# Batch 0's last couple in a fused attention and maxout kernel: two gate operations move ahead of four form operations, and one staged load moves behind two block turns

## The chip, the cores and the metric

The kernel runs on one core of a Trainium2 chip. The metric is device microseconds of that core, from the first to the last moment of one execution; several runs are taken and their median counts. A profile is one further execution, recorded instruction by instruction.

## The reference

For each of 8 batches, with S = 3072 tokens, D = 256 and 64 columns in z, a gated attention unit without softmax is computed, and its output goes through a maxout layer:

```python
scores = (1.0 / S) * np.matmul(z, z.transpose(0, 2, 1))
attn = np.maximum(scores, 0.0) ** 2
x = (u * np.matmul(attn, v)).reshape(B * S, D)          # 24576 x 256
out = np.maximum(x @ w1, x @ w2) @ w_out                # d_ff = 1024
```

All inputs and the output are float32 in HBM; the matmuls run in bf16.

## The kernel before

**Tiles.** The 3072 queries of a batch form six groups of 512, and a couple is two neighbouring groups, so a batch has three couples. The squared scores of one query group against four key tiles (512 keys) are a *block*, 128 partitions by 4 x 512 in bf16. Scores are symmetric, so only blocks with key index at or above the query index are computed; the others are *turned* copies, made by a DMA transpose (`mirror`, L279). There are 27 block buffers for everything. They stand in a list, `free`: `Block()` takes the first (L81), and `release()` puts a buffer at the end (L97). Both happen while the program is written out, not while it runs: `mirror` releases its source as soon as the turn has been put on the queue's list, and a later owner of that buffer gets a semaphore wait for the turn that still has to read it.

**Scores.** `score_pair` (L223) makes half a block: two matmuls into two of four PSUM banks (L237), ReLU by ScalarE into one of three `r_sb` buffers (L250; in every third pair of group 3 one half is done by VectorE, L248), and a square by VectorE into the block (L260). In group 3 of batch 0 one such pair is emitted at every fourth step of the attention matmuls (L297), and the pairs are those that later groups need.

**Batch 0.** Groups 0 to 3 are computed plainly (L297). Groups 4 and 5, batch 0's last couple, go by seven products of block sums (L1149), whose operands are *forms*: VectorE adds and subtracts whole blocks (L335, made by `prepare`, L337). For this couple `prepared(2)` gives 14 operations as `early`: eight on v (L193 to L196) and then, for the two forms, s3, s3, s1, s1, s2, s2. Each s1 reads a turned block. The *gate* of a group (L465, two operations for 512 queries) multiplies the attention output by the turned u and gives the feed-forward's input. Between group 3 and the couple, TensorE runs the feed-forward of couple 0 (L632 inner, L654 outer products).

**Order around the change.** Every engine runs its own list in order. SyncE's queue (SP) issues all turns, the staged loads and the stores. A staged load (`u_staged`, L207, and `z_staged`, L144, through `staged`, L129) takes a block buffer as float32 landing place, issues the load on SP, and has GpSimd cast it to bf16 (L142, L148). In group 3 (`i == 3`) the steps run over key tiles n; `u_staged(0, 5)` stands at n = 1, `z_staged` at n = 4, and a held-back turn (`later`) at n = 0, 4, 8, 12 and so on. After group 3, `sums` and the first `first` operations of `early` go to VectorE, then the gate of group 3, then the rest of `early`:

```python
        first = 4 * NC + len(forms)
        second(PLAIN // 2 - 2, sums + early[:first])
        xTs[b, g], gates = gate(b, g, {dc: h[0] for dc, h in halves.items()})
        for do in gates + early[first:]:
            do()
```

Here NC is 3 and there are two forms, so `first` is 14 and all of `early` stands ahead of the gate.

Of the kernel before, what the change touches and what calls it, by code (L numbers as in the profile page):

```python
# [11 lines left out]
def kernel(  # L12
# [26 lines left out]
    NC = NG // 2  # L39
# [79 lines left out]
    def zT_pe(lo, n, copies):  # L119
        tp = mm_tile([P, n, P], bf16, "tpz")[0]  # L120
        for j in range(n):
            nc.tensor.transpose(tp[:, j, :], z_bf16(lo + j - 1, 2), ident)  # L122
        at = 0
        for copy, k in copies:
            copy(zT[:, lo + at : lo + at + k, :], tp[:, at : at + k, :])
            at += k
        assert at == n
# [13 lines left out]
    def load_staged(dst, src):  # L141
        nc.gpsimd.tensor_copy(dst, staged(dst, src))  # L142
# [68 lines left out]
    def turn_u(b, g):  # L211
        t = upool.tile([P, G, KD, P], bf16, name="uT")
        nc.sync.dma_start_transpose(
            t.rearrange("p a c r -> p (a c) r"), un[b, g].rearrange("p a d -> p (a d)")
        )
        uT[b, g] = t
# [75 lines left out]
    def attn_unit(b, g, t, acc, dc, first, last):  # L292
        blk, j = divmod(t, G)
        a = A[b, g, blk]
        for half in range(2):
            rows = ds(half * R, R)
            nc.tensor.matmul(  # L297
                a.out(acc[half, dc]),
                v_at(b, t, dc)[rows],
                a.moving(rows, j),  # L300
                start=first,
                stop=last,
            )
        if dc == KD - 1 and j == G - 1:
            a.release()
# [4 lines left out]
    def drain(acc, dcs):  # L310
        hs = {}
        for dc in dcs:
            hs[dc] = new_h()
            nc.scalar.copy(hs[dc], acc[1, dc])
        for dc in dcs:
            nc.vector.tensor_add(hs[dc], hs[dc], acc[0, dc])
        return hs

    def drain_fast(acc, dc):
        hs = [new_h() for half in range(2)]  # L320
        nc.scalar.copy(hs[1], acc[1, dc])
        nc.vector.tensor_copy(hs[0], acc[0, dc])
        return hs
# [138 lines left out]
    def gate(b, g, hs):  # L462
        x = xpool.tile([P, KD, GW], bf16, name="xT")
        return x, [
            lambda dc=dc: nc.vector.scalar_tensor_tensor(  # L465
                out=x[:, dc, :].rearrange("p (t r) -> p t r", r=P),
                in0=hs[dc].rearrange("p (t r) -> p t r", r=P),
                scalar=c2,
                in1=uT[b, g][:, :, dc, :],
                op0=ALU.mult,  # L470
                op1=ALU.mult,
            )
            for dc in range(KD)
        ]
# [289 lines left out]
    def emit_pair(wait=0, shared=False, act=False):  # L764
        nonlocal done
        shared = shared or done < 12 and done % 3 == 0
        finish = score_pair(
            *pairs[done], dve_half=1 if shared else None, halves=done == 0, act=act
        )
        done += 1  # L770
        if wait:
            due.append((tick + wait, finish))
        else:
            finish()

    def flush(now=None):
        while due and (now is None or due[0][0] <= now):
            due.pop(0)[1]()
# [6 lines left out]
    def steps_of(i):  # L785
        tiles, both = range(NT), range(KD)
        head = edge(i - 1) if i else 0
        tail = NT - edge(i)
        steps = [(n, dc) for dc in both for n in tiles[:head]]
        steps += [(n, dc) for n in tiles[head:tail] for dc in both]  # L790
        return steps + [(n, dc) for dc in both for n in tiles[tail:]]
# [9 lines left out]
    def need(b, g, n):  # L801
        most = pair_at[b, g, 2 * g]
        for t in range(n + 1):
            if t // G >= g:
                most = max(most, pair_at[b, g, t // 2] + 1)
        return most

    with tc.manual_schedule():
# [21 lines left out]
        def by_chunk(w):  # L830
            return w.rearrange("(c p) f -> p c f", p=P)
# [32 lines left out]
        for i in range(PLAIN):  # L864
# [6 lines left out]
            for slot, (n, dc) in enumerate(steps_of(i)):  # L871
                k = need(b, g, n)
                upto = max(k, min(done + 1, k + AHEAD)) if slot in slots else k
                while done < min(upto, len(pairs)):
                    emit_pair(
                        wait=int(i < 2 and slot == slots[-1]), shared=i == 3 and done % 3 == 1
                    )
                if i == 0 and slot in (8, 22):
                    if slot == 8:
                        zT_pe(12, 8, [(nc.scalar.copy, 4)] * 2)  # L880
                    else:
                        zT_pe(20, 5, [(nc.scalar.copy, 5)])
                    if slot == 22:
                        for x in z_first:
                            x.release()
                attn_unit(b, g, n, acc, dc, n == 0, n == NT - 1)
                if n == NT - 1 and i < PLAIN - 1:
                    if i < 2:
                        new[dc] = drain_fast(acc, dc)
                        flush()  # L890
                    else:
                        new.update(drain(acc, [dc]))
                if dc:
                    continue
                if i in (1, 2) and n in (6, 9):
                    h = sums[n // 9]
                    nc.vector.tensor_add(h[0], h[0], h[1])
                    sums[n // 9] = h[0]
                if i and n == 12:
                    xTs[groups[i - 1]], tasks = gate(*groups[i - 1], sums)  # L900
                if i and n in (12, 15):
                    tasks[n // 15]()
                if i == 0 and n == 14:
                    turn_u(0, 0)
                if (i, n) == (0, 16):
                    turn_u(0, 1)
                if (i, n) == (0, 20):
                    nc.vector.memset(w2_sb[:, 0, 0:1], 0.0)
                    nc.gpsimd.dma_start(out=w2_sb, in_=by_chunk(moe_w2))
                if (i, n) == (1, 9):  # L910
                    w1_32 = [staged(w2_sb[:, c : c + 1], by_chunk(moe_w1)[:, c : c + 1]) for c in range(KD)]
                if (i, n) == (1, 11):
                    u_staged(0, 2)
                if (i, n) == (1, 13):
                    for h in range(2):
                        part = slice(h * KF // 2, (h + 1) * KF // 2)
                        load_staged(w_out_sb[:, part], by_chunk(moe_w_out)[:, part])
                if (i, n) in ((1, 15), (2, 14), (3, 4)):
                    z_staged(1, i - 1)
                if (i, n) == (2, 2):  # L920
                    turn_u(0, 2)
                if (i, n) == (2, 5):
                    u_staged(0, 3)
                if (i, n) == (2, 17):
                    turn_u(0, 3)
                if (i, n) in ((2, 18), (3, 1)):
                    u_staged(0, 4 + (i > 2))
                if (i, n) in ((2, 10), (3, 10)):
                    turn_z(1, i - 2)
                if (i, n) == (3, 16):  # L930
                    turn_z(1, 2)
                if later and n % 4 == 0 and (i == 3 or i and n > 12):
                    later.sort(key=lambda block: (block[2] > 3, block[1], block[2]))
                    mirror(*later.pop(0))
                if i == 2 and n == 16:
                    for c in range(KD):
                        nc.vector.tensor_sub(w15_sb[:, c : c + 1], w1_32[c], w2_sb[:, c : c + 1])
                if i == 2 and n in (15, 18):
                    half = n // 18
                    tp = mm_tile([P, KF, P], bf16, "tpw")[0]  # L940
                    for j in range(KF):
                        nc.tensor.transpose(tp[:, j, :], w2_sb[:, half, ts(j, P)], ident)
                    nc.scalar.copy(w2T_sb[:, half, :, :], tp)
                if i == 2 and n == 18:
                    w2.release()
# [66 lines left out]
        sums = [lambda h=h: nc.vector.tensor_add(h[0], h[0], h[1]) for h in halves.values()]  # L1012
        loads_behind(PLAIN // 2 - 1)
        forms, early, last_v, late = prepared(PLAIN // 2)
        first = 4 * NC + len(forms)
        second(PLAIN // 2 - 2, sums + early[:first])
        xTs[b, g], gates = gate(b, g, {dc: h[0] for dc, h in halves.items()})
        for do in gates + early[first:]:
# [3 lines left out]
        for i in range(PLAIN // 2, len(couples)):  # L1022
# [4 lines left out]
                b, c, forms, blocks=() if b else (q2, q1)  # L1027
# [102 lines left out]
            for s, pair in enumerate(steps):  # L1130
# [9 lines left out]
                for half, (name, w, blk, j) in enumerate(pair):  # L1140
                    rows = ds(half * R, R)
                    bank = BANK[name]
                    first = bank not in opened
# [28 lines left out]
            if i + 1 < len(couples):  # L1172
                forms, early, last_v, late = prepared(i + 1)
# [43 lines left out]
```

## Time and profile before

| | us |
|---|---|
| median of three runs | 902.83 (902.02 to 903.13) |
| the profiled execution itself | 904.61 |
| its span, first to last instruction | 902.6 |
| TensorE busy | 892.0 (99%) |
| VectorE busy | 741.7 (82%) |
| ScalarE busy | 722.6 (80%) |
| GpSimd busy | 95.4 (11%) |

Times inside the trace count from the span's start. The profiled execution took 1.78 us longer than the median of the runs, and 2.0 us of it lie outside the span. A timeline row gives start, duration, engine, line, operation and count, then in brackets how long the engine had been idle and what ended that. A row of SP (SPq) is the issue of a DMA; its landing comes later and is told by the view of one line.

### The profile page before, as it was taken

The numbers are of one execution on the slowest core, as the hardware profiler recorded it, in microseconds if no ns is written. First come the engines' busy times: TensorE is split into PE (matmuls) and PEld (weight loads), VectorE is DVE, ScalarE is ACT, GpSimd is POOL, SyncE is SP. The second block draws the span as 40 slices with busy tenths as digits, with TensorE's granted clock in tenths as the row PEclk, the third lists the DMA queues.
The fourth block names the chain that finished last, engine by engine and source line by source line (L and its number), as shares of the span: only waits on it lengthen the run. The fifth ranks groups of instructions, "written<-read, shape, count | busy, mean of one in ns | idle before, by whom it ended". The sixth has DMA issues, their size and how long they took to land.

```text
span 902.6 us, 19601 instructions
## 1 busy us (share of the span) xinstructions
PE 892.0 (99%) x7448; PEld 512.4 (57%) x7496; DVE 741.7 (82%) x1143; ACT 722.6 (80%) x1362; POOL 95.4 (11%) x176
## 2 busy tenths in 40 slices
PE   9999999999999999999999999999999999999998
PEld 4455656565565555655646556566465564555655
DVE  6897888988889887889798898988888988878732
ACT  7886879887888878888798887888879888794643
POOL 3211200201002010020101101011100110000000
PEclk9999999999999999999999999999999999999999
DMA  9999999999799996998999989799988999796301
GB/s 188 222 220 200 210 209 167 185 168 191 129 191 158 191 175 111 139 171 155 190 164 208 148 177 184 137 200 133 207 154 144 199 168 168 146 147 140 74 24 71
DMA packets 396014, 148.10 MB, mean 164 GB/s; under 512 B 361264, under 2 KB 375856, under 8 KB 395920
## 3 DMA queue, kind: packets, MB, share of 16 engines
q1 hardware_dynamic: 373488, 119.32, 73.2%
q0 software_dynamic: 22288, 27.40, 22.6%
q8 instruction: 58, 0.95, 0.4%
q14 instruction: 36, 0.29, 0.1%
q10 hardware_dynamic: 144, 0.13, 0.0%
HBM read 59.77 MB, written 25.17 MB: 94 GB/s over the span
## 4 chain that ended last, share of the span: by engine, by line
PE 93%; DVE 3%; DMA 2%; issue 1%; SPq 0%; ACT 0%; DVEq 0%
PE acc L1149 43%; PE acc L534 14%; PE acc L654 9%; PE d_ps L632 7%; PE s_ps L237 7%; PE d_ps L550 5%; PE d_ps L577 5%; PE acc L297 3%; DMA blk<-blk 2%; DVE blk L335 1%; DVE blk L260 1%; SPq L134 0%; DVE xT L465 0%; PE acc L842 0%; PE tpz L122 0%
## 5 line engine op out<-in xcount | busy, mean ns | idle before, releaser
L1149 PE MATMUL acc<-blk,v_sb 64*128 64x512 bf16 x2144 | 387.4, 376 | 0.1
L250 ACT ACTIVATE r_sb<-s_ps 128x512 bf16<-128x512 f32 (+3 forms) x661 | 329.4, 564 | 57.6 <-PE s_ps L237 49.3
L335 DVE TENSOR_TENSOR blk<-blk,blk 128x2048 bf16<-128x2048 bf16 x260 | 310.4, 1220 | 21.0 <-DMA blk<-blk 13.3
L1149 PE MATMUL acc<-blk,vt 64*128 64x512 bf16 x1560 | 317.1, 376 | 0.0
L1149 PEld LDWEIGHTS <-v_sb 64*128 64x128 bf16 x2144 | 152.8, 94 | 124.7 <-issue 4.9
L260 DVE TENSOR_TENSOR blk<-r_sb 128x1024 bf16<-128x1024 bf16 x196 | 134.9, 701 | 52.5 <-ACT r_sb L250 51.1
L1149 PEld LDWEIGHTS <-vt 64*128 64x128 bf16 x1560 | 124.4, 94 | 77.3 <-issue 3.3
L237 PE MATMUL s_ps<-zT 64*128 64x512 bf16 (+3 forms) x672 | 128.3, 358 | 1.8 <-DVE r_sb L248 1.6
L645 ACT ACTIVATE g_sb<-d_ps 128x512 bf16<-128x512 f32 x152 | 88.2, 602 | 46.2 <-PE d_ps L632 40.5
L534 PE MATMUL acc<-w_out_sb,g_sb 128*128 128x256 bf16 x896 | 118.4, 273 | 0.0
L534 PEld LDWEIGHTS <-g_sb 128*128 128x128 bf16 x896 | 87.6, 98 | 28.1
L654 PE MATMUL acc<-w_out_sb,g_sb 128*128 128x256 bf16 x632 | 93.3, 273 | 0.0
L632 PE MATMUL d_ps<-xT,w_sb 128*128 128x512 bf16 x300 | 89.1, 379 | 1.2 <-issue 0.2
L587 DVE TENSOR_TENSOR g_sb<-blk,d_ps 128x512 bf16<-128x512 f32 x84 | 56.0, 686 | 40.8 <-PE d_ps L577 40.3
L654 PEld LDWEIGHTS <-g_sb 128*128 128x128 bf16 x632 | 61.8, 98 | 34.9
L557 ACT ACTIVATE g_sb<-d_ps 128x512 bf16<-128x512 f32 x112 | 63.6, 605 | 13.7 <-PE acc L1149 9.7
L179 POOL DMA_DIRECT2D v_sb<-in_v_dram x90 | 48.0, 553 | 227.2 <-PE acc L1149 215.9
L1045 DVE TENSOR_TENSOR h_sb<-h_sb,acc 128x512 f32<-128x512 f32 x89 | 58.7, 681 | 6.7 <-PE acc L1149 6.7
L465 DVE SCALAR_TENSOR_TENSOR xT<-h_sb,uT 128x512 bf16<-128x512 f32 x96 | 60.7, 684 | 3.5 <-PE d_ps L632 3.5
L258 ACT ACTIVATE blk<-r_sb 128x1024 bf16<-128x1024 bf16 x59 | 62.5, 1059 | 1.3
L588 ACT ACTIVATE g_sb<-g_sb 128x512 bf16<-128x512 bf16 x84 | 50.9, 629 | 11.3 <-DVE g_sb L587 10.0
L550 PE MATMUL d_ps<-xT,w_sb 128*128 128x512 bf16 x210 | 59.2, 380 | 0.0
(89 smaller groups left out, 735.8 us busy)
## 6 DMA issues: line engine op xcount, KB each, us to landing
out_dram<-o_sb SPq DMA_DIRECT2D x95, 256.0 KB, 3.1
un<-in_u_dram POOLq DMA_DIRECT2D x44, 256.0 KB, 5.9
v_sb<-in_v_dram POOLq DMA_DIRECT2D x84, 128.0 KB, 6.8
blk<-blk SPq DMA_TRANSPOSE x240, 4.9
zn<-in_z_dram POOLq DMA_DIRECT2D x18, 128.0 KB, 5.0
blk<-in_u_dram SPq DMA_DIRECT2D x4, 512.0 KB, 5.0
v_sb<-in_v_dram POOLq DMA_DIRECT2D x6, 256.0 KB, 6.0
blk<-in_moe_w_dram SPq DMA_DIRECT2D x2, 512.0 KB, 4.3
```

The lines of the kernel that those rows point to most:

```text
L237: nc.tensor.matmul(s_ps[h][:, lo[h] :], zT[rows, z_at(b, blk * G + tiles[h], h), :], zT[rows, q + lo[h] // P : q + G, :].rearrange("p t c ...
L250: nc.scalar.activation(o, s, AF.Relu)
L258: nc.scalar.activation(a[:, k : k + 2, :], r, AF.Square)
L260: nc.vector.tensor_mul(a[:, k : k + 2, :], r, r)
L335: op(*((by_key(x) if mixed else x.ap) for x in blocks))
L534: nc.tensor.matmul(o_ps[key][:, t % 2, :], x[:, ts(t, P)], w, start=first, stop=stop and t % 2 == 1,)
L550: nc.tensor.matmul(d_ps, w15_sb[:, kc, ts(nb, P)], xs[q][:, kc, :], start=kc == 0, stop=kc == KD - 1,)
L557: nc.scalar.activation(new_g(q, name), d_ps, AF.Relu)
L632: nc.tensor.matmul(d_ps, w15_sb[:, kc, ts(nb, P)], xs[q][:, kc, :], start=(kc == 0), stop=(kc == KD - 1),)
L645: nc.scalar.activation(g_sb[q, nb], d_ps, AF.Relu)
L654: nc.tensor.matmul(o_ps[key][:, t % 2, :], x[:, ts(t, P)], w, start=first, stop=ends and (t % 2 == 1 or len(tiles) == 1) and n == len(weig ...
L1149: mm = nc.tensor.matmul(a.out(acc[name]), w()[rows], a.moving(rows, j), start=first, stop=left[name] == 0, skip_group_check=True,)
```

## The change

Two places. In group 3, the staged load of u for group 5 moves from key tile n = 1 to n = 9, behind the load of z at n = 4 and the turns at n = 4 and n = 8. And `first` becomes `len(early) - 2 * len(forms)`, which is 10: the two gates of group 3 now stand between s3, s3 and s1, s1, s2, s2 in VectorE's order.

```diff
                 if (i, n) == (2, 17):
                     turn_u(0, 3)
-                if (i, n) in ((2, 18), (3, 1)):
+                if (i, n) in ((2, 18), (3, 9)):
                     u_staged(0, 4 + (i > 2))
...
         forms, early, last_v, late = prepared(PLAIN // 2)
-        first = 4 * NC + len(forms)
+        first = len(early) - 2 * len(forms)
         second(PLAIN // 2 - 2, sums + early[:first])
```

## The prediction

> **What bounds the kernel now.** I read the page's first part, then TensorE's idle time by cause, then the order of time around the change on VectorE (DVE), SP and TensorE (PE).
>
> ```profile
> PE 892.0 (99%) x7448; PEld 512.4 (57%) x7496; DVE 741.7 (82%) x1143; ACT 722.6 (80%) x1362; POOL 95.4 (11%) x176
> ```
>
> PE is busy for 892.0 of 902.6 us, so the change can only win what PE idles. The waits from 71 to 95 us hold the one stall beyond 1 us that PE has after its start:
>
> ```profile
> DVE blk L335 <- DMA blk<-blk: 6.1, 2, 4.9
> PE s_ps L237 <- DVE r_sb L248: 1.6, 1, 1.6
> ```
>
> DVE's timeline shows where it comes from: two forms (s3), a wait of 4.92 us for a turned block, one s1, a wait of 1.13 us for a second, s1 and both s2, the two gates, one square, and only then the ReLU half (L248) for which PE waits.
>
> ```profile
> 71.97 2.35 DVE L335 TENSOR_TENSOR blk<-blk,blk 128x2048 bf16<-128x2048 bf16 x2
> 79.25 1.22 DVE L335 TENSOR_TENSOR blk<-blk,blk 128x2048 bf16<-128x2048 bf16 x1 [4.92 <-DMA blk<-blk]
> 81.60 3.50 DVE L335 TENSOR_TENSOR blk<-blk,blk 128x2048 bf16<-128x2048 bf16 x3 [1.13 <-DMA blk<-blk]
> 85.02 1.29 DVE L465 SCALAR_TENSOR_TENSOR xT<-h_sb,uT 128x512 bf16<-128x512 f32 x2
> ...
> 86.82 0.68 DVE L248 TENSOR_SCALAR r_sb<-s_ps 128x512 bf16<-128x512 f32 x1
> ```
>
> SP's timeline shows three turns, the load of u, the load of z, and the two turns in question; a turn's issue lasts as long as the transfer ahead of it, so SP is far behind the engines here.
>
> ```profile
> 62.75 8.54 SPq L281 DMA_TRANSPOSE blk<-blk  x3
> 71.39 0.54 SPq L134 DMA_DIRECT2D blk<-in_u_dram  x1
> 72.03 0.39 SPq L134 DMA_DIRECT2D blk<-in_z_dram  x1
> 72.47 6.85 SPq L281 DMA_TRANSPOSE blk<-blk  x2
> ```
>
> **The two edits by themselves.** Gates: two times 0.60 us (start to start) leave the path ahead of L248. PE's gap of 1.62 would shrink to 0.42. They can run there: their u was turned by the issue at 60.79 and their sums are done at 68.88. Load of u: on SP it is passed by the load of z and both turns. The first of these turns lands 6.7 us after 72.47, at 79.2, the second 4.3 us after 77.23, at 81.6. Without u ahead (its landing, 76.7, is 3.3 us behind the landing of the turn before it, 73.3) both come about 3.3 us earlier, near 75.8 and 78.3. Together, DVE would be through s2 near 82 and PE's 1.62 us would be gone. The load itself lands at about 81 us. On GpSimd its cast (1.04 us) now follows that of z, and behind it stand the v loads, the first of which waits for PE until 83.5: covered by 1 us, and the turn of this u is issued only at 93.37: covered.
>
> **What else the move does.** `u_staged` takes a block buffer, and `free` is a queue. At n = 1 of group 3 the first free buffer is blk11, released a little earlier by a `mirror` at n = 20 of group 2, which reads it. In the kernel before, u takes it; on SP the load stands behind that turn anyway. In the changed kernel nothing takes it at n = 1, so the score pair at n = 4 gets it, and the order of the built programs shows it (numbers are buffers):
>
> ```
> before  DVE L260 blk0  <- r_sb   waits for the turn blk5  <- blk0   (issued at 46.45)
> after   DVE L260 blk11 <- r_sb   waits for the turn blk14 <- blk11  (issued at 62.75)
> ```
>
> A square on DVE now waits for the first of the three turns of the row at 62.75. When does DVE want to run it? It is the first of the two at 54.70:
>
> ```profile
> 53.92 0.68 DVE L248 TENSOR_SCALAR r_sb<-s_ps 128x512 bf16<-128x512 f32 x1
> 54.70 1.47 DVE L260 TENSOR_TENSOR blk<-r_sb 128x1024 bf16<-128x1024 bf16 x2
> ...
> 59.79 0.69 DVE L260 TENSOR_TENSOR blk<-r_sb 128x1024 bf16<-128x1024 bf16 x1 [0.39 <-ACT r_sb L250]
> 60.40 0.68 DVE L465 SCALAR_TENSOR_TENSOR xT<-h_sb,uT 128x512 bf16<-128x512 f32 x1
> 61.00 0.68 DVE L248 TENSOR_SCALAR r_sb<-s_ps 128x512 bf16<-128x512 f32 x1
> ```
>
> And the view of L281 around 62.8 gives that turn's landing:
>
> ```profile
> L281 SPq DMA_TRANSPOSE blk<-blk x1: 3668/3668/3668, 62.8 to 62.8; - x1
> ...
> DMA to landing us min/median/max: 5.7/5.7/5.7
> ```
>
> Landing 62.75 + 5.7 = 68.45, and DVE starts about 0.1 later (79.17 to 79.25 above): 68.55 instead of 54.70. Nothing ahead of that turn on SP depends on the stalled work (its predecessors are turns of finished blocks and loads), so it does not move.
>
> **From DVE's stall to PE.** Queued behind the square on DVE: all later squares, two gates, every third pair's L248. PE is covered for a while. Call the stalled pair P0. There are three r_sb buffers, so ScalarE can fill P1 and P2, but P3 needs P0's buffer. There are four banks, two for a pair, so PE can still write P3 and P4, and stops at P5, which needs P3's banks. PE's rows stand 1.08 us apart; P0 is at 52.86, P5 at 58.26:
>
> ```profile
> 57.18 0.38 PE L237 MATMUL s_ps<-zT 64*128 64x512 bf16 x2
> ...
> 58.26 0.38 PE L237 MATMUL s_ps<-zT 64*128 64x512 bf16 x2
> 58.48 1.03 PE L297 MATMUL acc<-blk,v_sb 64*128 64x512 bf16 x8
> ```
>
> P3's first bank is freed by ScalarE: square done at 68.55 + 0.69 = 69.24, plus 0.60 is 69.85. Its second bank by DVE's L248, which stands behind three squares: 68.55 + 3 x 0.60 = 70.35, plus 0.69 is 71.05. PE's second matmul starts 0.05 later (87.51 to 87.56 at the old gap), at 71.10, and the attention matmuls at 71.11 instead of 58.48: **+12.6**. Behind it DVE and ScalarE have the next pairs' tiles ready, so PE meets no second wait: P8, at 71.1 + 3 x 1.08 = 74.3, needs an L248 that six DVE operations later ends at about 74.2.
>
> **What the delay gives back.** Everything on PE behind 58 us now comes some 12.6 later, while SP goes on. DVE reaches s1 at about 87, the turns land near 76 and 78: no wait, and the stall of 1.62 is gone, **-1.6**. PE's only other gap behind it is 0.1 (at 136.9). Both intended gains are thus contained in this -1.6 and cannot be had twice.
>
> **The clock.** PE would idle 11 us. The trace has two places to judge by. At the start, from 0.99 to about 6.8 us, matmuls run at half speed: the score matmul at 6.36 takes 0.56 where those above take 0.38. At the end, the clock granted from 901.0 to 902.6 is 0.51 (the number behind the five engines' busy times in the row by window) while PE's last matmul ended at 898.2:
>
> ```profile
> 6.36 0.56 PE L237 MATMUL s_ps<-zT 64*128 64x512 bf16 x2
> ```
>
> ```profile
> 901.00:902.60 1.60, 0.00 (x0) 0.00 (x0) 0.00 (x0) 0.00 (x0) 0.00 (x0) 0.51 0.00 0
> ```
>
> So 2.8 us of idling were enough to halve the clock, and up to 5.8 us of work ran before it came back. Half speed for 5.8 us costs 2.9; the lower end is 0, if the grant holds. PE had holes in that first stretch and would work densely here, so I take a little under the upper end: **+2.2**. [...]
>
> **Sum.** 12.6 - 1.6 + 2.2 = +13.2. The profiled execution would have a span of 902.6 + 13.2 = 915.8 and take 917.8; the runs' median lies 1.78 lower than the profiled time, at 902.83 + 13.2 = **916.0**.
>
> **Rivals.**
> 1. *The stall without the clock's loss.* The grant holds or PE's slow stretch hides behind DVE. Then +11.0: 913.8. For it: the clock's return is seen once in this trace. Against: 2.8 us were enough at the end. 0.17.
> 2. *What the edit says and no more.* The square finds blk11 free. PE's 1.62 us go: 901.2, a gain. Its condition: P3's L248 must be done by 58.2, so by the steps above (0.1 + 3 x 0.60 + 0.69 + 0.05) the turn must land by 55.6 instead of 68.45. Nothing in the change makes SP's list up to that turn shorter, so this needs the wait to be on another transfer than the one I read. 0.06.
> 3. *A longer stall*, over 918.5: the clock needs a second such stretch, or the later turns, released in a bunch, hold up the couple. 0.04.
> 4. *Nothing measurable*: the stall just eats the gain, which needs the landing at about 57. 0.01.
>
> **Numbers.** The forecast has 0.72. The range takes in the stall's landing (a turn lands 4.3 to 6.7 us after its issue in these rows, so -1.4 to +1.0) and the clock (0 to 2.9): 912.5 to 918.5, with rivals 2 to 4 outside. A difference under 0.2% (1.8 us) is about what a measurement cannot tell from none. Faster 0.06, same 0.02, slower 0.92.
>
> **What would show it.** Right: DVE's L260 idle for about 13 us until about 68.5, ended by the DMA; PE's L237 idle for about 11 us at 58 to 60, with slower matmuls for some us behind; no wait of L335 for a DMA near 79 plus the shift, and no gap before the couple's second pair. Wrong: a square at 54.70 as before. The clock step is wrong if matmuls behind the gap take 0.38 us at once.

## The result, and the profile after

The changed kernel takes 915.83 us (median of five runs, 913.35 to 916.1), 1.0131 times the kernel before (95% interval 1.0116 to 1.0146). The profiled execution is the one of 915.83 us. It was run a second time as it is, beside three experiments on another chip:

> The changed kernel once more, as the measure for the next three on the same chip: 915.8 us (913 to 916.5).

It took 915.02 us there (913.85 to 915.58), 1.0132 times the kernel before (1.0118 to 1.0146). Here and below a ratio is taken against the kernel before as it ran on the same chip beside it; its medians there are 902.83 to 903.15 us.

TensorE's row on the page: 3.6 us more busy time, although the work is the same, and a span that is 11.5 us longer than 902.6.

```profile
span 914.1 us, 19650 instructions
...
PE 895.6 (98%) x7496; PEld 509.5 (56%) x7496; DVE 742.9 (81%) x1143; ACT 722.7 (79%) x1362; POOL 96.8 (11%) x176
```

The waits from 50 to 110 us (engine and line, what it waited for, us in total, times, longest) show one chain of three waits of nearly the same length, and no L335 that waits for a DMA:

```profile
DVE blk L260 <- DMA blk<-blk: 14.5, 1, 14.5
ACT r_sb L250 <- DVE blk L260: 13.4, 1, 13.4
...
PE s_ps L237 <- ACT r_sb L250: 12.1, 1, 12.1
...
PE s_ps L237 <- DVE r_sb L248: 0.5, 1, 0.5
```

Read from the top: VectorE's square waits for a turn, ScalarE's ReLU for that square (its `r_sb`), TensorE's score matmul for that ReLU (its bank). On VectorE's timeline the square that stood at 54.70 is now at 67.63:

```profile
52.41 0.68 DVE L248 TENSOR_SCALAR r_sb<-s_ps 128x512 bf16<-128x512 f32 x1
67.63 1.89 DVE L260 TENSOR_TENSOR blk<-r_sb 128x1024 bf16<-128x1024 bf16 x3 [14.53 <-DMA blk<-blk]
69.44 0.68 DVE L248 TENSOR_SCALAR r_sb<-s_ps 128x512 bf16<-128x512 f32 x1
...
85.96 2.35 DVE L335 TENSOR_TENSOR blk<-blk,blk 128x2048 bf16<-128x2048 bf16 x2
88.23 1.28 DVE L465 SCALAR_TENSOR_TENSOR xT<-h_sb,uT 128x512 bf16<-128x512 f32 x2
89.44 4.62 DVE L335 TENSOR_TENSOR blk<-blk,blk 128x2048 bf16<-128x2048 bf16 x4
```

The last three rows are the couple's forms: s3, s3, the gates, then s1, s1, s2, s2 back to back. The 4.92 and 1.13 us that they waited before are gone, as the change says. SP's timeline shows the turn that the square waits for (the first of three in its first row), the load of z, the two turns of the forms, and only then the load of u:

```profile
61.70 8.54 SPq L281 DMA_TRANSPOSE blk<-blk  x3
70.29 0.68 SPq L134 DMA_DIRECT2D blk<-in_z_dram  x1
71.07 4.55 SPq L281 DMA_TRANSPOSE blk<-blk  x2
75.67 1.29 SPq L134 DMA_DIRECT2D blk<-in_u_dram  x1
```

The view of that first turn names who waits for it, and its landing:

```profile
L281 SPq DMA_TRANSPOSE blk<-blk x1: 3728/3728/3728, 61.7 to 61.7; - x1
...
  DVE blk L260: 14.5, 1
...
DMA to landing us min/median/max: 5.8/5.8/5.8
```

TensorE's timeline across the stall, and its row by window behind it (us; busy time of PE, PEld, DVE, ACT, POOL, each with its instructions; granted clock; DMA share; GB/s):

```profile
55.67 0.38 PE L237 MATMUL s_ps<-zT 64*128 64x512 bf16 x2
55.89 1.03 PE L297 MATMUL acc<-blk,v_sb 64*128 64x512 bf16 x8
69.06 0.58 PE L237 MATMUL s_ps<-zT 64*128 64x512 bf16 x1 [12.14 <-ACT r_sb L250]
70.17 0.58 PE L237 MATMUL s_ps<-zT 64*128 64x512 bf16 x1 [0.53 <-DVE r_sb L248]
70.18 2.28 PE L297 MATMUL acc<-blk,v_sb 64*128 64x512 bf16 x8
```

```profile
71.00:74.00 3.00, 3.00 (x18) 1.24 (x16) 2.59 (x5) 0.99 (x2) 0.23 (x1) 0.50 1.03 229
74.00:76.00 2.00, 2.00 (x16) 0.93 (x14) 2.00 (x3) 1.09 (x2) 1.39 (x2) 0.67 0.82 178
76.00:80.00 4.00, 4.00 (x34) 1.83 (x31) 3.09 (x6) 2.93 (x6) 0.00 (x0) 1.00 1.08 250
```

Eight attention matmuls take 2.28 us behind the gap and 1.03 ahead of it; the clock is 0.50 at first and full again by 76 us. So "busy" rose in part because the same matmuls ran slower. The larger part of the 3.6 us is no time of the kernel: the page of before has 7448 matmul records against 7496 here, and its trace has 48 holes of 0.05 us in TensorE's row, 2.5 us together, where the records are missing. The other 1.1 us agree with the next paragraph: 2.5 us for a slower stretch behind the stall, less 1.5 us at the start.

**Where the 11.5 us are**, by comparing the start of the same TensorE instruction in the two traces. Before the stall the changed kernel is 1.5 us *ahead* (the pair's row at 57.18 is at 55.67). That is no effect of the change: the records of the clock show full speed from 3.65 us on, and from 6.73 in the profiled execution of before; the score pair at 4.56 us takes 0.39 us in the one, the pair at 4.74 takes 0.61 in the other. The stall: the attention row at 58.48 starts at 70.18, +11.7, so +13.2 against that lead. The slow clock: from there to the couple's first inner product takes 8.88 us instead of 6.37, +2.5. The old gap of 1.62, gone: -1.8 around 87 us. The remaining -0.9 comes in pieces under 0.5 further on. The sum is +11.5 for the two profiled executions, +13.0 without the start's lead; the medians differ by 13.0.

### The profile page after: what moved, and what is told of

Its sections match the earlier page's. It is cut to its first block, busy times and chain, and to the rows that moved or that the text cites. A ratio compares the mean times of both kernels' runs of the same rounds, so it can differ in the third digit from the quotient of the medians.

```text
span 914.1 us, 19650 instructions
## 1 busy us (share of the span) xinstructions
PE 895.6 (98%) x7496; PEld 509.5 (56%) x7496; DVE 742.9 (81%) x1143; ACT 722.7 (79%) x1362; POOL 96.8 (11%) x176
## 4 chain that ended last, share of the span: by engine, by line
PE 92%; DMA 1%; DVE 0%; issue 0%; SPq 0%; DVEq 0%
PE acc L1149 44%; PE acc L534 13%; PE acc L654 9%; PE d_ps L632 8%; PE s_ps L237 6%; PE d_ps L550 5%; PE d_ps L577 5%; PE acc L297 1%; DMA blk<-blk 1%; PE acc L704 0%; DVE blk L260 0%; DVE r_sb L248 0%; SPq L134 0%; DVE o_sb L728 0%; SPq L213 0%
## 5 line engine op out<-in xcount | busy, mean ns | idle before, releaser
L250 ACT ACTIVATE r_sb<-s_ps 128x512 bf16<-128x512 f32 (+3 forms) x661 | 329.2, 563 | 68.5 <-PE s_ps L237 54.0
L335 DVE TENSOR_TENSOR blk<-blk,blk 128x2048 bf16<-128x2048 bf16 x260 | 310.0, 1219 | 8.3 <-PE acc L1149 6.3
L632 PE MATMUL d_ps<-xT,w_sb 128*128 128x512 bf16 x320 | 92.0, 379 | 0.0
L237 PEld LDWEIGHTS <-zT 64*128 64x128 bf16 x672 | 36.0, 94 | 50.4 <-issue 13.1
L550 PE MATMUL d_ps<-xT,w_sb 128*128 128x512 bf16 x224 | 62.2, 380 | 0.0
```

Of the source, the lines that this page charges most:

```text
L237: nc.tensor.matmul(s_ps[h][:, lo[h] :], zT[rows, z_at(b, blk * G + tiles[h], h), :], zT[rows, q + lo[h] // P : q + G, :].rearrange("p t c ...
L250: nc.scalar.activation(o, s, AF.Relu)
L335: op(*((by_key(x) if mixed else x.ap) for x in blocks))
L550: nc.tensor.matmul(d_ps, w15_sb[:, kc, ts(nb, P)], xs[q][:, kc, :], start=kc == 0, stop=kc == KD - 1,)
L632: nc.tensor.matmul(d_ps, w15_sb[:, kc, ts(nb, P)], xs[q][:, kc, :], start=(kc == 0), stop=(kc == KD - 1),)
```

## The experiments

The theory to test: the whole loss is the buffer that the moved load leaves in `free`; the gates have no part in it; about 2 us of the loss are the clock. Rivals: the load's new place on SP costs something of its own (a later transfer, a longer stall elsewhere); the gates' new place costs something; the gap costs only its own length.

**One edit at a time.** The load moved, and the order of gates and forms as before:

```diff
-        first = len(early) - 2 * len(forms)
+        first = 4 * NC + len(forms)
```

> Only the load of u moves; the gates stay behind all 14 operations. Theory (the block buffer that the load no longer takes goes to a score pair, whose square then waits for a turn still in the queue): all of the loss is here, 915 us (913.5 to 917), VectorE's square idle for 14 to 15 us. Rival A (the four form operations behind the gates come too late for the couple): the loss is in the gates, so about 902 us here.

Measured: 914.81 us (913.79 to 915.89), ratio 1.0128 (1.0115 to 1.0142): the whole loss. VectorE's square waits 13.7 us for its turn, just under the 14 to 15 expected, and TensorE 11.3 us for L250. Then the gates alone:

```diff
-                if (i, n) in ((2, 18), (3, 9)):
+                if (i, n) in ((2, 18), (3, 1)):
```

> Only the gates move; the load stays at key tile 1. Theory: no stall of the square; TensorE's gap of 1.62 us shrinks by the two gates of 0.60 to about 0.4, so 901.6 us (900.5 to 902.5). Rival A: 913 us or more.

Measured: 902.19 us (900.93 to 908.27, twelve runs), ratio 0.9997 (0.9982 to 1.0011): no difference to be told. The gates did what the edit says: L335 still waits for its turns, but the gates are through, and TensorE's gap there is smaller, though 0.9 us and not the 0.4 expected (these are the waits of this kernel from 71 to 100 us; before it was 1.6).

```profile
DVE blk L335 <- DMA blk<-blk: 5.7, 2, 4.5
PE s_ps L237 <- DVE r_sb L248: 0.9, 1, 0.9
```

**The buffer alone.** In the kernel before, the first two entries of `free` change places just ahead of the load of u; neither the load nor a gate moves. u takes the second buffer, and the score pair gets blk11:

```diff
+                if (i, n) == (3, 1):
+                    free[0], free[1] = free[1], free[0]
                 if (i, n) in ((2, 18), (3, 1)):
                     u_staged(0, 4 + (i > 2))
```

> The kernel before, in its old order; only the first two free buffers change places at key tile 1 of group 3, so that the load takes blk0 and the score pair takes blk11. Theory: the same stall as in the changed kernel with none of its edits, +13 us less the recovered gap, 915.5 us (913.5 to 917). Rivals A and B: no edit, no loss, 902.8 us.

Measured: 914.55 us (913.84 to 916.45), ratio 1.0129 (1.0113 to 1.0144). Exchanging two names in a list costs all that the change costs, with the same two waits:

```profile
DVE blk L260 <- DMA blk<-blk: 13.3, 1, 13.3
...
PE s_ps L237 <- ACT r_sb L250: 10.9, 1, 10.9
```

**The change without the buffer.** Now the changed kernel, with blk11 sent to the end of `free` where u used to take it:

```diff
+                if (i, n) == (3, 1):
+                    free.append(free.pop(0))
                 if (i, n) in ((2, 18), (3, 9)):
                     u_staged(0, 4 + (i > 2))
```

> The whole change, but at key tile 1 of group 3 the first free buffer is put at the end of the list, so that the score pair gets the same buffer as before the change. Theory: no stall of the square, and what the two edits are worth by themselves shows: TensorE's gap of 1.62 us gone, 901.2 us (900 to 902.3), faster than both. Rival B (the load of u behind two turns, or what it delays on SyncE and GpSimd, is what costs): still 913 to 916 us.

Measured: 904.89 us (901.31 to 909.45, twelve runs), ratio 1.0026 (1.0006 to 1.0045). The stall of the square is gone, and so is the old gap: TensorE's largest idle in this stage is 0.28 us. But the executions scatter over 8 us, and the median is not the 901.2 that the prediction gave for "what the edit says and no more". The same kernel without the gates' part:

```diff
+                if (i, n) == (3, 1):
+                    free.append(free.pop(0))
...
-        first = len(early) - 2 * len(forms)
+        first = 4 * NC + len(forms)
```

> Only the load of u moves, with the buffer put at the end of the list as in the version with the buffer aside. By the prediction's figures the turns land 3.3 us earlier and the gap of 1.62 us goes without the gates: 901.2 us (900 to 902.3). If the earlier turns are worth nothing by themselves: 902.8.

Measured: 902.13 us (900.8 to 903.31), ratio 0.9989 (0.998 to 0.9997).

**A later turn.** If the landing of one transfer sets the stall, a buffer whose turn lands later must move the end by as much. The changed kernel with the newest entry of `free` (blk19, source of the third turn in SP's row at 61.70) put first for the pair:

```diff
+                if (i, n) == (3, 1):
+                    free.insert(0, free.pop())
```

> The changed kernel, but the score pair is given blk19, whose turn is the third of the three in the queue and lands 4.8 us behind that of blk11 (72.3 against 67.5 in the changed kernel's trace). Theory: the landing sets the stall's end one for one, so 4.8 us over the changed kernel, 920.6 (919 to 922). If anything else than that landing sets the end: about 915.8.

Measured: 920.18 us (918.97 to 920.68), ratio 1.0189 (1.0175 to 1.0203), 5.2 above the changed kernel beside it. In the two profiles of that chip the turn that the square waits for lands at 71.39 instead of 66.19, 5.2 us later, so the landing does set the end one for one. VectorE's timeline has the same rows as above, with the square later still:

```profile
52.47 0.68 DVE L248 TENSOR_SCALAR r_sb<-s_ps 128x512 bf16<-128x512 f32 x1
71.51 1.90 DVE L260 TENSOR_TENSOR blk<-r_sb 128x1024 bf16<-128x1024 bf16 x3 [18.36 <-DMA blk<-blk]
```

**The clock.** The gap filled with 50 matmuls on a zero operand:

```diff
+                if i == 3 and slot == 24:
+                    for fill in range(50):
+                        nc.tensor.matmul(acc[0, 0], zeros, w_out_sb[:, 0:2, :]..., start=False, stop=False, ...)
```

> The changed kernel with 50 matmuls of zero weights (they add zero to an open accumulator) ahead of the sixth score pair, about 10.8 us of work inside TensorE's stall. Theory (half speed behind the stall costs 2.3 to 2.5 us of the 13): the remaining idle time is about 1.4 us, the clock stays granted, matmuls behind it take 0.38 us, and the time is 2.4 us under the changed kernel, 913.4 against 915.8. Rival C (VectorE and ScalarE set the pace behind the stall, and the clock costs nothing): no difference, 915.8.

Measured: 913.16 us (912.81 to 913.76), ratio 1.0114 (1.0098 to 1.0129), 1.9 below the changed kernel beside it. The stall ends at the same place, and the matmuls behind it are fast at once, at a granted clock of 1.00 from 58 to 80 us (row of the filler, then as above):

```profile
56.87 10.74 PE L878 MATMUL acc<-w_out_sb,zeros 128*128 128x512 bf16 x49 [0.16 <-issue]
68.95 0.37 PE L237 MATMUL s_ps<-zT 64*128 64x512 bf16 x1 [1.34 <-ACT r_sb L250]
70.07 0.37 PE L237 MATMUL s_ps<-zT 64*128 64x512 bf16 x1 [0.74 <-DVE r_sb L248]
70.08 1.23 PE L297 MATMUL acc<-blk,v_sb 64*128 64x512 bf16 x8
```

So this gap on TensorE costs its length and about 1.9 us more.

**Why the change without the buffer wins nothing.** Both kernels with the buffer aside were run again:

> The version with the buffer aside again, for the profile of one of its slower executions (903 to 909 us, granted clock 0.993 to 0.998). Theory (what was gained at 86 us is given back where couple 1's turns end: the form operation there waits longer for a turn, TensorE idles over 2.5 us and loses the clock): gaps of TensorE between 115 and 135 us, summing with the slower stretch to the excess over 901.3. Rival: the loss is elsewhere, near 60 us or in the later batches.

> As the run before it: a third profile of the same version, since its time varies between executions; the excess over 901.3 us is expected in gaps of TensorE between 115 and 135 us.

> The load alone with the buffer aside again: 902.1 us (901 to 903), 0.1% under the kernel before, and no execution over 904. If it shares the slower executions of the version with both edits: some at 905 to 909.

With the gates moved: 907.61 us (two executions, 905.96 and 909.26), ratio 1.0055 (1.0035 to 1.0075), then 903.9 (902.12 to 908.23, eight executions), ratio 1.0018 (1.0002 to 1.0035). Without: 903.16 (901.16 to 905.88), ratio 1.0008 (0.9997 to 1.0019), with three of eleven executions over the 904 that was expected as the most. So the 0.9989 of the first time did not come again, and no version here is shown to beat the kernel before.

The profiled execution of the second run, 909.26 us, shows where its gain is lost, as was expected. At the instruction that stands at 87.56 us in the kernel before, TensorE is 2.8 us ahead of it, about 1 us of that from the start as above. Then SP's timeline has

```profile
92.11 8.34 SPq L213 DMA_TRANSPOSE uT<-un  x2
100.54 27.62 SPq L281 DMA_TRANSPOSE blk<-blk  x8
```

where the first run of the same kernel, profiled in an execution of 901.31 us, has

```profile
89.64 6.25 SPq L213 DMA_TRANSPOSE uT<-un  x2
95.98 27.78 SPq L281 DMA_TRANSPOSE blk<-blk  x8
```

The couple's next forms read turns of that row of eight. In the second run their L335 on VectorE waits 7.14 us, TensorE waits for it twice, 2.32 and 1.67 us, and the granted clock is 0.50 from 124 to 134 us, where the first run has 1.00 (VectorE, then TensorE, then the windows):

```profile
123.12 1.23 DVE L335 TENSOR_TENSOR blk<-blk,blk 128x2048 bf16<-128x2048 bf16 x1 [7.14 <-DMA blk<-blk]
```

```profile
124.40 1.01 PE L1151 MATMUL acc<-blk,v_sb 64*128 64x512 bf16 x3 [2.32 <-DVE blk L335]
...
128.38 0.58 PE L1151 MATMUL acc<-blk,v_sb 64*128 64x512 bf16 x1 [1.67 <-DVE blk L335]
```

```profile
124.00:134.00 10.00, 7.93 (x39) 3.61 (x40) 9.83 (x19) 2.01 (x5) 0.82 (x2) 0.50 0.93 219
```

In the first run that form starts at 116.44, in the kernel before at 119.30, and TensorE waits for it in neither. The execution of the gates alone that was profiled, 907.31 us, has the same picture: a wait of 9.13 us until 122.01, a TensorE gap of 2.73 until 127.27, and behind it matmuls of 0.63 us that took 0.38 ahead of it (mean granted clock 0.83 from 124 to 134 us). So in these two executions TensorE comes to this place sooner than in the kernel before, and the turn lands later.

That TensorE comes sooner is not enough by itself. With the load alone and the buffer aside it is 2.0 and 2.7 us ahead at the same instruction in the two profiles, yet none of the 22 executions of that version took over 906 us, and none of the 64 of the kernel before. With the gates alone 2 of 12 did, with both edits 8 of 22. These long executions thus go with the moved gates; by what path is not shown.

The third run, whose profiled execution of 905.03 us has no such gap, lost most of its time a batch later. A row of six turns on SP starts at 213.92 there and at 209.17 in the first run, a form waits 6.61 us for one of them until 230.19, and TensorE goes from 1.6 us ahead of the kernel before to 0.9 behind between 235 and 249 us, at full clock (1.000 over that execution). What stays open is why SP falls back in some executions of the same program. Between the second run and the first the lag is 0.5 us at 44 us, 1.2 at 84 and 4.6 at the row of eight. In the changed kernel's profile the second and third issue of the row at 61.70 end at 67.74 and 70.24, and the transfers ahead of them landed at 67.50 and 70.05: each of these issues lasted until about the landing ahead of it, which fits a lag that is handed on, but does not show what adds to it.

## Why the prediction was right

**The buffer** held as written: the square waits for the turn of the row at 62.75 (now 61.70), which landed at 67.50, 5.8 us after its issue against 5.7 read from the trace of before. The buffers exchanged in the kernel before give the loss without the change, the buffer aside takes it away, a later turn makes it longer.

**The path from VectorE to TensorE** held at each station: ScalarE waits for the square, TensorE for ScalarE at the pair that was named, then shortly for L248. The stall was put at 12.6 and is 13.2 when the lead of 1.5 at the start is taken out. The turn landed about 1 us earlier than the 68.45 of the sum, which alone would make the stall shorter; TensorE came 1.5 us earlier still. The difference of 0.6 is that of the two.

**The gap recovered** was put at -1.6 and is -1.8, as contained in the stall and not beside it.

**The clock** was put at +2.2, between 0 and 2.9. The trace has +2.5 for the rows to the end of the group. The second profile of the same kernel has +1.7 for the same rows (8.06 us instead of 6.37), those of the load alone, the buffers exchanged and the later turn +1.5 to +1.8, and filling the gap won 1.9 (with 2.1 us of idling left). Dense work behind the gap ran at half speed for 5.2 us in the first profile (70.18 to 75.33) and for 3.5 in the second (68.86 to 72.38). Both are under the 5.8 us that the prediction read from the start of the trace of before, and the price of 2.9 at its upper end was not reached. Rival 1, which had no such loss, fell with this.

**The sum** of 13.2 met 13.0 partly by luck: the stall and the clock of that execution came out 0.9 us above their terms, and small pieces of 0.9 us, which the prediction did not have, took it back.

**What was off** is a side estimate: rival 2's price of 901.2 for the two edits without the buffer. Its step is that TensorE's 1.62 us go and all else stays. With the buffer aside the gap did go, but the median was 903.9 to 907.6 in three runs, since in some executions TensorE then waits for later rows of turns. The prediction looked for such waits behind the stall (a gap of 0.1 at 136.9), not in the case without it. The price of the gates alone was off too: they were to leave 0.42 us of the gap of 1.62, and left 0.9.

## What to carry to other kernels

Where buffers come from one list in the order of the program text, moving a load also hands its buffer to somebody else; follow the buffer numbers and the waits of the built program, not only the order of instructions. A buffer released when a transfer that reads it is put on a queue, not when it lands, is fine for a taker that stands behind it on that queue (the load of u into blk11, issued at 71.39 us in the kernel before, behind that turn's issue at 62.75) and expensive for an engine that does not (VectorE waited 14.5 us here). Price a TensorE gap with the slower matmuls behind it (1.9 us beside a gap of 12.14 us here), and before counting a gap as won, look at the next transfers that the work will then reach sooner, and at how much their landing varies (the row of eight turns began at 95.98 us in one execution and at 100.54 in another of the same program).

## What the runs showed of the hardware

The granted clock as recorded: in the kernel before it is full from 6.73 to 901.02 us, the gap of 1.62 us included, and half from there to the end of the span; TensorE's last matmul had ended at 898.2. In the changed kernel it is full from 3.65 to 61.68 us, half from there to 75.33 (13.65 us), and full again to the end of the span. TensorE's gap of 12.14 us runs from 56.92 to 69.06 there, so the clock fell 4.8 us into the gap and came back 6.3 us behind it. The means over the profiled executions are 0.999 for the kernel before, 0.993 for the changed kernel and for the load alone, 0.994 for the buffers exchanged, 0.991 for the later turn and 1.000 with the gap filled. So the 1.62 us cost no clock, and the stall did; what sets the lengths of the half stretches is not shown.

The start differs between executions: full speed is on record from 6.73 us in the profile of the kernel before and from 3.65 in that of the changed one, and TensorE is 1.5 us ahead in the second at the pair that stands at 57.18 in the first. That may be most of the 1.8 us by which the profiled execution of before lies above its median (an estimate: the starts of the other executions are not on record), and it is a reason not to compare two single executions to better than that.
